# Batch 0's attention output in another pair of PSUM banks and in one piece, w_out decoded early and used split from the first chunk, splits made in place

## The chip, the cores and the metric

One core of one Trainium2 chip runs the whole kernel as one launch. The time is device time in microseconds (us); lower is better. The engines spoken of are PE (TensorE: matmuls and transposes), ACT (ScalarE), DVE (VectorE) and SP (SyncE, which issues every DMA here, in order). Each engine works through its own queue in order and waits on semaphores of the others.

## The reference, cut to what matters

```python
# attention: 2 batches, 8 heads, 768 positions, head size 64, 16 clusters per head
q_assign = argmax(q_n @ c_n.T); k_assign = argmax(k_n @ c_n.T)
mask = q_assign[..., :, None] == k_assign[..., None, :]
scores = where(mask, scale * q @ k.T, -1e9)
attn = softmax(scores); attn_out = attn @ v
x = attn_out.transpose(0, 2, 1, 3).reshape(1536, 512)
# first expert: w_in 512x2048, w_out 2048x512
h = x @ w_in
g = (a0 + a1*h + a2*h**2 + a3*h**3) / (1 + |b0|*|h| + |b1|*h**2 + 1e-6)
x = g @ w_out
# second expert: w1, w2 512x1024, w3 1024x1024, w_out 1024x512
out = ((x @ w1) * (x @ w2) @ w3) @ w_out2
```

All in fp32; the weights reach the kernel as 64-bit floats, two 32-bit words per number.

## The kernel before, in words

**Order.** The program doesn't write its order out by hand. It lists tasks (`op(engine, cost, fn, reads, writes, priority)`), and `Plan.order` places them by fixed costs over 19 rounds. The numbers in `CFG` (`AT`, `LEAD`, `OFF`, `T0` and so on) set the first round's priorities. What comes out is one order per engine and one slot for every buffer; a buffer class such as `w` has a fixed number of slots (`SLOTS`), and a new buffer waits until the slot's last user is done.

**Attention.** A head of a batch is six units (`Attn.unit`): four matmul passes give a 128x768 tile of scores in PSUM class `s` (L791), DVE takes the row maximum (L799), ACT the exponential with its sum (L800), PE turns the tile by six transposes into class `t` in two lots of three (L813), and ACT copies each lot out (L816). After six units `Attn.av` transposes the inverse sums (L833, tile R) and multiplies by v (L849, tile o), both in class `t`, whose two banks the transposes use too. The product is three tasks of four matmuls, so the planner may put other work between them. Batch masks (`masks`) come from cluster products (L415), counts (L435) and DVE passes (L426 to L438).

**Experts.** Tokens go through in four chunks of 384 columns, c = 0 to 3, each in blocks of eight 128-row steps: `p1_block` (w_in, PSUM class `s`), `p2_block` (w_out, class `m`), `p3_block` (w1 and w2, `m`), `p4_block` (w3 times w_out2, `m`). w3 times w_out2 is formed once (`FirstW`, L581, and `w_block`, L597, stored to `whd`/`wld` by `w_out_part`, L548 and L549). Chunks 0 and 1 are batch 0, chunks 2 and 3 batch 1.

**Two kinds of product.** A block of kind `D` uses the fp32 weight itself: one matmul per 128-row step, which the chip runs as two instructions (L536). Other kinds split weight and operand into a rounded high part and a low part (hi and lo, type fp32r) and make three matmuls: hi x hi, hi x lo, lo x hi (L538, L539, L540). The matrices named in `F0` are `D` in chunk 0, where w_in and w_out are used in fp32 as they come out of `decode` (ACT L466, DVE L467, L468, L470). The decoded weights are also stored to DRAM (`fin`, `fout`, `f12`); the later chunks load them (kind `S`) into a `raw` buffer, ACT rounds them to hi (L501) and DVE subtracts to get lo (L502), both in class `w`, which has 6 slots; `raw` has 3, and `p1_block`'s temporary V uses them as well.

```python
    F0=("in", "out"),
            elif k == "S":
                self.f = Buf("raw", [P, WB])
                dma(lambda: self.f.t, self.full[0], 524288, ...)
            self.hi, self.lo = Buf("w", [P, WB], F32R), Buf("w", [P, WB], F32R)
```

Of the kernel before, what the change touches and what calls it, by code (L numbers as in the profile page):

```python
# [9 lines left out]
F32 = mybir.dt.float32  # L10
# [11 lines left out]
    F0=("in", "out"),  # L22
    SPLIT=7,
    NW=(1, 3),
    AT=(0.0, 1.125, 2.5, 2.5, 3.6667, 4.0, 4.0),
    M1=0,
    LEAD=(-21.2, 10.4, -104.0),
    ALEAD=(37.3, 148.2),
    MLEAD=16.4,
    AOFF=-83.5,  # L30
    SLOTS={"w": 6, "raw": 3, "y": 3, "x": 2, "x2": 2, "g": 21, "et": 3, "E": 4, "kqr": 1, "A": 2, "B": 2, "v": 1, "sm": 6, "nn": 3, "s": 2, "t": 2, "m": 2, "sums": 2, "rb": 1},
    WO2=-2226.6,
    OFF=(-156.1, -36.7, -5.3, -214.6, -121.6, 36.6, -69.0),
# [254 lines left out]
def kernel(  # L288
# [34 lines left out]
    if not only_plan:  # L323
# [9 lines left out]
        f_d = {n: dr.tile([8, P, WB], F32, name="f" + n) for n in ("in", "out", "12")}  # L333
        ident = cst.tile([P, P], F32, name="ident")
# [138 lines left out]
    class Blk:  # L473
# [7 lines left out]
        def prep(self):  # L481
            k, at = self.kind, self.at
            pl, psp = at - cfg["LEAD"][0 if k != "L" else 1] - (0 if k == "L" else cfg["LEAD"][1]), at - cfg["LEAD"][1]
            if k in "DE":
                self.f = Buf("w", [P, WB])
                raws = [load_raw(self.src, i, at - cfg["LEAD"][2]) for i in range(2)]
                for i in range(2):
                    decode(raws[i], lambda i=i: self.f.t[:, i * HB:(i + 1) * HB], (self.f, i), psp)
                if self.full is not None:
                    dma(lambda: self.full[0](), lambda: self.f.t, 524288, [(self.f, 0), (self.f, 1)], [self.full[1]], at)  # L490
                if k == "D":
                    return
            elif k == "S":
                self.f = Buf("raw", [P, WB])
                dma(lambda: self.f.t, self.full[0], 524288, [self.full[1]], [(self.f, 0), (self.f, 1)], pl)
            self.hi, self.lo = Buf("w", [P, WB], F32R), Buf("w", [P, WB], F32R)
# [539 lines left out]
```

## Time and profile before

| | |
|---|---|
| median of 3 runs | 811.92 us (811.42 to 814.1) |
| the profiled execution's own time | 808.21 us |
| its span, first to last instruction | 806.4 us |
| busy: PE, DVE, ACT | 781.4, 608.3, 555.5 us |
| mean granted TensorE clock | 0.996 of 2.4 GHz |
| moved by DMA | 147.69 MB |

Busy time is the union of an engine's instructions; PE's matmuls overlap, so what a matmul costs is read from the distance between starts, not from its duration. A wait is idle time put down to the semaphore that came last.

### The profile page before, as it was taken

To read this page: it belongs to the slowest core of one execution; us is meant where nothing else is said; L and a number is where in the kernel's file an instruction comes from. 1 tells how busy PE (TensorE), PEld (TensorE's weight loads), DVE (VectorE), ACT (ScalarE), POOL (GpSimd) and SP (SyncE) were. 2 spreads that over 40 slices of the span, in tenths; PEclk is the share of its full clock that TensorE was granted. 3 is DMA by queue.
4 is the path that set the end of the run, shared out by engine and by line. 5 is a ranking of instruction groups with operands and counts; after the bars stand their busy time and mean duration, and the time that the engine had idled before them with its cause. 6 is when DMAs were issued, how large, how long until landed. Compare 5 with 4: busy or idle time off the path is not lost.

```text
span 806.4 us, 11425 instructions
## 1 busy us (share of the span) xinstructions
PE 781.4 (97%) x4225; PEld 638.7 (79%) x4225; DVE 608.3 (75%) x826; ACT 555.5 (69%) x943; POOL 0.7 (0%) x6
## 2 busy tenths in 40 slices
PE   5989999998989999999999999999999999999998
PEld 1446656665655667588888899999999999999998
DVE  5977888866479999779999847389967397975440
ACT  7579887877777897389988836287945386863331
POOL 0000000000000000000000000000000000000000
PEclk9999999999999999999999999999999999999999
DMA  8996747767334347973435665414475332655334
GB/s 331 323 330 183 250 154 228 247 186 235 129 109 152 101 146 236 316 261 114 161 119 162 225 211 179 143 69 151 169 250 172 105 118 94 225 186 176 130 104 145
DMA packets 54344, 147.69 MB, mean 183 GB/s; under 512 B 5904, under 2 KB 23056, under 8 KB 54288
## 3 DMA queue, kind: packets, MB, share of 16 engines
q1 hardware_dynamic: 54288, 146.96, 54.8%
q8 instruction: 33, 0.54, 0.3%
q14 instruction: 23, 0.19, 0.1%
HBM read 119.15 MB, written 24.64 MB: 178 GB/s over the span
## 4 chain that ended last, share of the span: by engine, by line
PE 80%; ACT 7%; DVE 6%; DMA 5%; issue 1%; SPq 0%; DVEq 0%; ACTq 0%
PE m L539 12%; PE m L538 12%; PE m L540 12%; PE t L849 7%; PE s L791 6%; PE t L813 6%; PE m L536 5%; PE s L538 4%; PE s L540 4%; PE s L539 4%; PE m L597 3%; PE s L536 3%; ACT E L800 1%; DMA kqr<-in_kq_dram 1%; ACT et L816 1%
## 5 line engine op out<-in xcount | busy, mean ns | idle before, releaser
L502 DVE TENSOR_TENSOR w<-raw,w 128x1024 fp32r<-128x1024 f32 x72 | 87.9, 1222 | 43.5 <-ACT w L501 42.6
L540 PE MATMUL m<-g,w 128*128 128x384 f32 x320 | 107.9, 337 | 0.0
L538 PE MATMUL m<-g,w 128*128 128x384 f32 x320 | 107.8, 337 | 0.0
L539 PE MATMUL m<-g,w 128*128 128x384 f32 x320 | 107.7, 337 | 0.0
L501 ACT CAST w<-raw 128x1024 fp32r<-128x1024 f32 x72 | 75.5, 1050 | 46.3 <-PE m L539 35.2
L816 ACT COPY et<-t 128x384 f32<-128x384 f32 x192 | 88.7, 503 | 22.0 <-PE t L813 21.9
L799 DVE TENSOR_REDUCE sm<-s 128x1 f32<-128x768 f32 x96 | 90.3, 949 | 14.0 <-PE s L791 13.8
L800 ACT ACTIVATE E<-s,sm 128x768 f32<-128x768 f32 x96 | 88.8, 929 | 10.9 <-DVE sm L799 9.7
L813 PEld LDWEIGHTS t<-ident,E 128*128 128x128 f32 x576 | 69.2, 141 | 30.5 <-issue 11.9
L813 PE MATMUL t<-ident,E 128*128 128x128 f32 x576 | 86.4, 277 | 4.4 <-ACT et L816 3.2
L538 PE MATMUL m<-x,w 128*128 128x384 f32 x256 | 87.3, 341 | 0.0
L539 PE MATMUL m<-x,w 128*128 128x384 f32 x256 | 86.3, 337 | 0.0
L540 PE MATMUL m<-x,w 128*128 128x384 f32 x256 | 85.6, 334 | 0.0
L849 PE MATMUL t<-et,v 128*64 128x384 f32 x384 | 68.5, 494 | 0.0
L538 PE MATMUL s<-x,w 128*128 128x384 f32 x192 | 66.3, 345 | 0.9 <-DVE et L657 0.9
L791 PE MATMUL s<-A 128*128 128x384 f32 x192 | 60.1, 394 | 6.2 <-ACT E L800 5.6
L540 PE MATMUL s<-x,w 128*128 128x384 f32 x192 | 64.9, 338 | 0.0
L539 PE MATMUL s<-x,w 128*128 128x384 f32 x192 | 64.4, 335 | 0.0
L466 ACT ACTIVATE y<-raw 128x512 f32<-128x512 f32 x66 | 45.5, 698 | 25.8 <-DMA raw<-in_w_out_dram 10.6
L539 PEld LDWEIGHTS m<-g,w 128*128 128x128 f32 x320 | 60.1, 188 | 0.0
L538 PEld LDWEIGHTS m<-g,w 128*128 128x128 f32 x320 | 60.1, 188 | 0.0
L540 PEld LDWEIGHTS m<-g,w 128*128 128x128 f32 x320 | 60.1, 188 | 0.0
(122 smaller groups left out, 1468.6 us busy)
## 6 DMA issues: line engine op xcount, KB each, us to landing
kqr<-in_kq_dram SPq DMA_DIRECT2D x16, 768.0 KB, 4.7
raw<-fin SPq DMA_DIRECT2D x24, 512.0 KB, 3.4
raw<-fout SPq DMA_DIRECT2D x24, 512.0 KB, 3.4
raw<-f SPq DMA_DIRECT2D x24, 512.0 KB, 3.2
raw<-in_w3t_dram SPq DMA_DIRECT2D x16, 512.0 KB, 5.9
raw<-in_w_in_dram SPq DMA_DIRECT2D x16, 512.0 KB, 4.9
raw<-in_w_out_dram SPq DMA_DIRECT2D x16, 512.0 KB, 3.9
raw<-in_w_dram SPq DMA_DIRECT2D x16, 512.0 KB, 4.7
```

What stands on the lines that cost most here:

```text
L501: op("ACT", 0.95, lambda: nc.scalar.copy(self.hi.t, self.f.t), [(self.f, 0), (self.f, 1)], [self.hi], psp)
L502: op("DVE", 1.135, lambda: nc.vector.tensor_tensor(self.lo.t, self.f.t, f32(self.hi.t), ALU.subtract), [(self.f, 0), (self.f, 1), self.hi] ...
L536: nc.tensor.matmul(o, w.f.t[:, sl], x[0], start=first, stop=last)
L538: nc.tensor.matmul(o, w.hi.t[:, sl], x[0], start=first, stop=False)
L539: nc.tensor.matmul(o, w.hi.t[:, sl], x[1], start=False, stop=False)
L540: nc.tensor.matmul(o, w.lo.t[:, sl], x[0], start=False, stop=last)
L791: nc.tensor.matmul(p.t[:, f, 0:TA], lhs.t[0:n, q0:q0 + P], lhs.t[0:n, k0:k0 + TA], start=st, stop=not st)
L799: op("DVE", 0.865, lambda: nc.vector.tensor_reduce(mx.t, p.t[:, :, 0:TA], axis=AX.XY, op=ALU.max, negate=True), [p], [mx], OF[1])
L800: op("ACT", 0.88, lambda: nc.scalar.activation(E.t, p.t[:, :, 0:TA], AF.Exp, bias=mx.t, accum_out=sums.t[:, i, j:j + 1]), [p, mx], [E, (su ...
L813: nc.tensor.transpose(t.t[:, n * P:(n + 1) * P], e[:, kt * P:(kt + 1) * P], ident)
L816: op("ACT", 0.371, lambda t=t, lot=lot: nc.scalar.copy(et.t[:, 3 * lot:3 * lot + 3, i * P:(i + 1) * P], t.t[:, 0:TA].rearrange("p (a b) -> ...
L849: nc.tensor.matmul(o.t[64 * j:64 * j + 64, 0:TA], v.t[:, kt, h % 2, :], ets[j].t[:, kt, :], start=kt == 0, stop=kt == NKT - 1)
```

## The change

It does five things. (1) `F0` loses `"out"`: chunk 0's w_out blocks become split blocks, and chunk 0's g is kept as hi and lo. (2) `PRE=("out",)`: w_out is decoded and stored to DRAM by eight blocks of its own (`early`), placed from `PT` on in the attention stage, and chunk 0 loads it back like the later chunks. (3) A split block loads its float weight into the `w` buffer that becomes lo; DVE subtracts in place, and no `raw` buffer is used. (4) `AVP=("m", "t")`: batch 0's R and o use class `m`, the expert layers' two banks, and the product with v is one task per head. (5) The priorities are other numbers. `KEEP={}` and `ETV=(0.0, 0.0)` leave their new branches unused.

```diff
-    F0=("in", "out"),
-    SPLIT=7,
-    NW=(1, 3),
-    AT=(0.0, 1.125, 2.5, 2.5, 3.6667, 4.0, 4.0),
+    F0=("in",),
+    KEEP={},
+    PRE=("out",),
+    PT=(-39.8, 52.4),
+    ETV=(0.0, 0.0),
+    AVP=("m", "t"),
+    EF="w",
+    SPLIT=8,
+    NW=(1, 4),
+    AT=(0.9167, 3.0, 3.125, 4.0, 4.0, 4.0, 4.0),
...
+            if k == "F":
+                self.f = Buf("w", [P, WB])
+                dma(lambda: self.f.t, self.full[0], 524288, [self.full[1]], [(self.f, 0), (self.f, 1)], pl)
+                return
             if k in "DE":
-                self.f = Buf("w", [P, WB])
+                self.f = f = Buf("w" if k == "D" else cfg["EF"], [P, WB])
+            if k != "D":
+                self.lo = Buf("w", [P, WB], F32R)
+            if k in "SL":
+                f = self.lo
+            words = [(f, 0), (f, 1)]
...
             elif k == "S":
-                self.f = Buf("raw", [P, WB])
-                dma(lambda: self.f.t, self.full[0], 524288, [self.full[1]], [(self.f, 0), (self.f, 1)], pl)
-            self.hi, self.lo = Buf("w", [P, WB], F32R), Buf("w", [P, WB], F32R)
+                dma(lambda: f32(f.t), self.full[0], 524288, [self.full[1]], words, pl)
+            self.hi = Buf("w", [P, WB], F32R)
...
-                op("ACT", 0.95, lambda: nc.scalar.copy(self.hi.t, self.f.t), [(self.f, 0), (self.f, 1)], [self.hi], psp)
-                op("DVE", 1.135, lambda: nc.vector.tensor_tensor(self.lo.t, self.f.t, f32(self.hi.t), ALU.subtract),
-                   [(self.f, 0), (self.f, 1), self.hi], [self.lo], psp)
+                op("ACT", 0.95, lambda: nc.scalar.copy(self.hi.t, f32(f.t)), words, [self.hi], psp)
+                op("DVE", 1.135, lambda: nc.vector.tensor_tensor(self.lo.t, f32(f.t), f32(self.hi.t), ALU.subtract),
+                   words + [self.hi], [self.lo], psp)
...
+        if c == 0 and n in cfg["PRE"]:
+            early.append(Blk("D", src, full))
+            return Blk("F" if n in F0 else "S", None, full, parts if n not in F0 and keep < NCH else None)
...
-            sums, rb, R = self.sums[h], Buf("rb", [P, NQT, P]), Buf("t", [P, 512])
+            bank = cfg["AVP"][b]
+            sums, rb, R = self.sums[h], Buf("rb", [P, NQT, P]), Buf(bank, [P, 512])
...
-            o = Buf("t", [P, 512])
+            o = Buf(bank, [P, 512])
...
-            for k0 in range(0, NKT, 2):
-                lots = {k // 3 for k in (k0, k0 + 1)}
-                op("PE", 1.31, lambda k0=k0: q(k0), [v] + [(e, l, i) for e in ets for l in lots for i in range(NQT)], [o], at)
+            op("PE", 4.06, q, [v] + [(e, l, i) for e in ets for l in range(2) for i in range(NQT)], [o], at)
```

What the change does to the order is seen at three places. In the rows, a name such as `g_2881` is a buffer of class g with a running number, `x2` counts repeats, and lines of the changed kernel are shifted (L849 becomes L883, L813 becomes L843, L799 becomes L829).

PE at the first head's product with v (`o` and R; transposes of E between): before,

```order
L833 MATMUL t_603<-ident,rb_594 128x128 x3
L849 MATMUL t_611<-et_492,v_318 64x384
L849 MATMUL t_611<-et_552,v_318 64x384
L849 MATMUL t_611<-et_492,v_318 64x384
L849 MATMUL t_611<-et_552,v_318 64x384
L813 MATMUL t_619<-ident,E_581 128x128 x3
L849 MATMUL t_611<-et_492,v_318 64x384
L849 MATMUL t_611<-et_552,v_318 64x384
L849 MATMUL t_611<-et_492,v_318 64x384
L849 MATMUL t_611<-et_552,v_318 64x384
```

and in the changed kernel:

```order
L867 MATMUL m_703<-ident,rb_694 128x128 x3
L843 MATMUL t_711<-ident,E_680 128x128 x3
L843 MATMUL t_715<-ident,E_680 128x128 x3
L883 MATMUL m_719<-et_564,v_429 64x384
L883 MATMUL m_719<-et_645,v_429 64x384
L883 MATMUL m_719<-et_564,v_429 64x384
L883 MATMUL m_719<-et_645,v_429 64x384
L883 MATMUL m_719<-et_564,v_429 64x384
```

The transposes of E no longer stand inside the product, R and o have moved from the `t` banks to `m`, and over the whole order the product is in 16 stretches where it was in 30.

DVE just ahead of the first row maximum (TENSOR_REDUCE of `sm`), before,

```order
L470 SCALAR_TENSOR_TENSOR x_381<-w_310,y_378 128x512
L470 SCALAR_TENSOR_TENSOR w_420<-raw_365,y_399 128x512
L549 TENSOR_TENSOR raw_448<-t_236,w_439 128x512
L799 TENSOR_REDUCE sm_453<-s_434 128x1
L799 TENSOR_REDUCE sm_458<-s_443 128x1
```

and in the changed kernel, where L433 to L445 are mask work and L474, L477 decoding:

```order
L433 TENSOR_TENSOR g_493<-g_461,s_452 128x768
L477 SCALAR_TENSOR_TENSOR x_404<-w_397,y_443 128x512
L445 SCALAR_TENSOR_TENSOR g_431<-s_476,g_418 128x768
L434 STREAM_TRANSPOSE g_499<-g_493 128x768
L474 TENSOR_SCALAR y_491<-y_491 128x512
L435 TENSOR_REDUCE nn_514<-g_499 128x48
L829 TENSOR_REDUCE sm_518<-s_502 128x1
L829 TENSOR_REDUCE sm_522<-s_509 128x1
```

Nine of batch 1's twelve DVE mask passes now stand ahead of the first row maximum; before they all stood far behind it (batch 0's twelve are ahead in both). On PE, the cluster products of batch 1 and one of its two counts have moved there too, and 28 of `FirstW`'s 32 matmuls stand ahead of the first unit where 30 did.

PE in chunk 0's w_out blocks (`g` times `w` into `m`), before,

```order
L536 MATMUL m_2989<-g_2227,w_2954 128x384 x2
L536 MATMUL m_2989<-g_2318,w_2954 128x384 x2
L536 MATMUL m_2989<-g_2411,w_2954 128x384 x2
L536 MATMUL m_2989<-g_2477,w_2954 128x384 x2
L536 MATMUL m_2989<-g_2549,w_2979 128x384 x2
```

and in the changed kernel:

```order
L568 MATMUL m_3344<-g_2881,w_3371 128x384
L569 MATMUL m_3344<-g_2897,w_3371 128x384
L570 MATMUL m_3344<-g_2881,w_3298 128x384
L568 MATMUL m_3344<-g_2881,w_3371 128x384
L569 MATMUL m_3344<-g_2897,w_3371 128x384
L570 MATMUL m_3344<-g_2881,w_3298 128x384
```

One matmul per step has become three, with a second g buffer and a second w buffer. The slots that the order gives to class `w` have moved as well: among the last 64 blocks that ACT and DVE split, the slot for hi is free one PE block ahead of its first matmul for 53 and two blocks ahead for 11, and the slot for lo three blocks ahead for 51. Before, both slots were mostly free two blocks ahead.

## Rows read from the trace of the kernel before

**Rows 1.** The page's first part: busy time, share of the span and instructions of each engine.

```profile
PE 781.4 (97%) x4225; PEld 638.7 (79%) x4225; DVE 608.3 (75%) x826; ACT 555.5 (69%) x943; POOL 0.7 (0%) x6
```

**Rows 2.** Busy time by stage: the stretch, its length, then busy us and instructions of PE, PE's weight loads, DVE, ACT and POOL, granted TensorE clock, DMA share and GB/s.

```profile
0.00:58.00 58.00, 46.54 (x159) 19.65 (x160) 44.00 (x83) 38.66 (x60) 0.70 (x6) 0.97 0.95 335
58.00:84.00 26.00, 24.67 (x144) 17.55 (x143) 20.19 (x29) 25.65 (x58) 0.00 (x0) 1.00 0.65 191
...
177.00:203.00 26.00, 22.05 (x121) 15.26 (x120) 18.11 (x28) 20.81 (x47) 0.00 (x0) 0.93 0.76 237
...
240.00:322.00 82.00, 81.66 (x371) 54.22 (x370) 78.03 (x110) 69.23 (x125) 0.00 (x0) 1.00 0.49 155
322.00:347.00 25.00, 25.00 (x95) 13.99 (x94) 19.81 (x33) 9.58 (x15) 0.00 (x0) 1.00 0.93 310
347.00:445.00 98.00, 95.86 (x581) 83.15 (x580) 90.72 (x125) 86.28 (x156) 0.00 (x0) 1.00 0.49 159
445.00:803.00 358.00, 358.00 (x2057) 354.96 (x2055) 240.78 (x284) 203.25 (x281) 0.00 (x0) 1.00 0.47 159
```

**Rows 3.** The chain that ended last, one piece of chunk 0's w_out blocks (start us, length us, what, instructions); and PE's groups by line and shape: instructions, then busy us and mean ns of one.

```profile
321.24 19.35 PE m L536 x60
```

```profile
L536 PE MATMUL m<-g,w 128*128 128x384 f32 x128 | 43.6, 486 | 0.0
```

**Rows 4.** Timeline of PE around the end of one split block and the whole next one (start us, length us, engine, line, operation, tiles, shape, count): L539 is the last reader of a block's hi.

```profile
479.80 0.34 PE L539 MATMUL m<-g,w 128*128 128x384 f32 x1
...
480.15 0.34 PE L538 MATMUL s<-x,w 128*128 128x384 f32 x1
...
484.36 0.34 PE L538 MATMUL m<-g,w 128*128 128x384 f32 x1
```

**Rows 5.** Timeline of PE at two heads' products with v: one in two pieces with a lot of transposes between, one in a single piece.

```profile
67.06 1.51 PE L849 MATMUL t<-et,v 128*64 128x384 f32 x8
68.50 0.55 PE L813 MATMUL t<-ident,E 128*128 128x128 f32 x3
68.98 2.80 PE L849 MATMUL t<-et,v 128*64 128x384 f32 x16
71.71 0.55 PE L813 MATMUL t<-ident,E 128*128 128x128 f32 x3
...
84.32 4.09 PE L849 MATMUL t<-et,v 128*64 128x384 f32 x24
88.34 0.62 PE L791 MATMUL s<-A 128*128 128x384 f32 x2
```

**Rows 6.** The start on DVE: busy time of DVE in a stretch (its length, busy us and instructions, then clock and DMA), then its timeline at the first row maxima, where square brackets give idle time and who ended it.

```profile
10.44:49.30 38.86, 38.45 (x68) 0.96 0.97 358
```

```profile
48.66 0.70 DVE L470 SCALAR_TENSOR_TENSOR w<-raw,y 128x512 uint32<-128x512 uint32 x1
52.59 0.69 DVE L549 TENSOR_TENSOR raw<-t,w 128x512 fp32r<-128x512 f32 x1 [3.24 <-ACT w L548]
53.20 1.81 DVE L799 TENSOR_REDUCE sm<-s 128x1 f32<-128x768 f32 x2
```

**Rows 7.** Pieces of the chain that ended last: batch 1's cluster products and counts, and `FirstW`'s matmuls (two instructions each).

```profile
21.56 1.72 PE t L581 x4
...
109.45 1.43 PE s L415 x16
...
116.95 1.29 PE s L435 x4
```

**Rows 8.** Who waited for whom from 184 to 190 us (us in total, times, longest), and single microseconds of the same stretch in the columns of the table by stage.

```profile
DVE w L470 <- DMA whd<-w: 3.5, 1, 3.5
...
PE s L791 <- ACT E L800: 2.5, 2, 2.1
```

```profile
188.00:189.00 1.00, 0.47 (x1) 0.47 (x2) 0.96 (x3) 1.00 (x4) 0.00 (x0) 0.70 0.01 4
189.00:190.00 1.00, 1.00 (x5) 0.90 (x5) 0.64 (x1) 0.55 (x2) 0.00 (x0) 0.50 1.07 283
190.00:191.00 1.00, 1.00 (x6) 1.00 (x5) 0.79 (x1) 0.82 (x3) 0.00 (x0) 0.50 1.09 197
191.00:192.00 1.00, 1.00 (x6) 1.00 (x5) 0.17 (x1) 0.81 (x2) 0.00 (x0) 0.59 0.82 188
```

**Rows 9.** Timeline of ACT and of DVE where one block's weight is split: ACT waits for the slot of hi, then rounds; DVE subtracts.

```profile
480.17 1.05 ACT L501 CAST w<-raw 128x1024 fp32r<-128x1024 f32 x1 [2.75 <-PE m L539]
```

```profile
481.25 1.22 DVE L502 TENSOR_TENSOR w<-raw,w 128x1024 fp32r<-128x1024 f32 x1 [2.08 <-ACT w L501]
```

**Rows 10.** DVE's groups by line and shape (instructions, then busy us and mean ns of one): the three passes of a decode, and the split of g.

```profile
L468 DVE SCALAR_TENSOR_TENSOR y<-raw,y 128x512 uint32<-128x512 uint32 x66 | 45.0, 685 | 0.7
L470 DVE SCALAR_TENSOR_TENSOR w<-raw,y 128x512 uint32<-128x512 uint32 x64 | 43.7, 686 | 10.0 <-DMA whd<-w 3.5 <-PE s L536 2.3 <-DMA f<-w 2.2
...
L467 DVE TENSOR_SCALAR y<-y 128x512 uint32<-128x512 uint32 x72 | 30.0, 419 | 9.9 <-ACT y L466 9.8
L530 DVE TENSOR_TENSOR g<-et,g 128x768 fp32r<-128x768 f32 x24 | 22.9, 953 | 1.8 <-ACT g L528 1.8
```

**Rows 11.** DMA issues of the page: engine queue, operation, count, KB each, median us from issue to landing.

```profile
raw<-fout SPq DMA_DIRECT2D x24, 512.0 KB, 3.4
```

More of the change, by code (lines that the diff above doesn't have):

```diff
@@ L333 @@
         f_d = {n: dr.tile([8, P, WB], F32, name="f" + n) for n in ("in", "out", "12")}
+        s_d = {n: dr.tile([2, 8, P, WB], F32, name="s" + n) for n in ("in", "out", "12")}
         ident = cst.tile([P, P], F32, name="ident")
@@ L510, in cost @@
         def cost(self, n):
-            return n * (0.645 if self.kind == "D" else 0.523)
+            return n * (0.645 if self.kind in "DF" else 0.523)
     def moe_blk(c, n, i, src):
         full = (lambda: f_d[n][i], ("f", n, i))
-        if c == 0:
-            return Blk("D" if n in F0 else "E", src, full)
-        return Blk("S", None, full)
+        parts = tuple((lambda j=j: s_d[n][j, i], [("s", n, i, j)]) for j in range(2))
+        keep = cfg["KEEP"].get(n, 9)
+        if c == 0 and n in cfg["PRE"]:
+            early.append(Blk("D", src, full))
+            return Blk("F" if n in F0 else "S", None, full, parts if n not in F0 and keep < NCH else None)
+        if c == 0:
+            if n in F0:
+                return Blk("D", src, full)
+            return Blk("E", src, full if keep > 1 else None, parts if keep < NCH else None)
+        if c >= keep:
+            return Blk("L", None, None, parts)
+        return Blk("S", None, full, parts if n in F0 and c == 1 and keep < NCH else None)
+    early = []
     def operand(n, cls, shape, c):
@@ L815, in unit @@
                 op("PE", 0.327, tr, [E], [t], OF[3])
[L816 to L818 removed]
+                u, part = 6 * h + qt, cfg["ETV"][self.b]
+                on_dve = lot == 1 and int(part * (u + 1)) > int(part * u)
+                op("DVE" if on_dve else "ACT", 0.43 if on_dve else 0.371,
+                   lambda t=t, lot=lot, v=on_dve: (nc.vector.tensor_copy if v else nc.scalar.copy)(
+                       et.t[:, 3 * lot:3 * lot + 3, i * P:(i + 1) * P], t.t[:, 0:TA].rearrange("p (a b) -> p a b", a=3)),
+                   [t], [(et, lot, i)], OF[4])
             if qt == 2 * NQT - 1:
@@ L842, in av, with q @@
             op("PE", 0.327, tr, [rb], [R], at)
-            o = Buf("t", [P, 512])
+            o = Buf(bank, [P, 512])
             ets = [self.et[h, 0], self.et[h, 1]]
-            def q(k0):
-                for kt in range(k0, k0 + 2):
+            def q():
+                for kt in range(NKT):
                     for j in range(2):
@@ L914 @@
         clock += tm + ta
+    for i, b in enumerate(early):
+        b.at = cfg["PT"][0] + i * cfg["PT"][1]
+        events.append((b.at, 1, "pre", b))
     events.sort(key=lambda e: (e[0], e[1]))
@@ L919, with decode_early @@
     mask_at = {e[3]: e[0] for e in events if e[2] == "mask"}
-    state = {"b": 0, "h": 0, "u": 0, "m": []}
+    state = {"b": 0, "h": 0, "u": 0, "e": 0, "m": []}
+    def decode_early(key):
+        for b in early[state["e"]:]:
+            if key is not None and ("f", *key) in plan.wr:
+                break
+            b.prep()
+            state["e"] += 1
+            if key is None:
+                break
     def prep_blocks(i):
         while state["b"] <= min(i, len(blocks) - 1):
+            if blocks[state["b"]].kind in "FS":
+                decode_early(blocks[state["b"]].full[1][1:])
             blocks[state["b"]].prep()
```

38 lines of the change are left out of this document (21 added, 17 removed).

## The prediction

> **What bounds the kernel now.** I read the page's busy shares first: PE is busy 781.4 us of a span of 806.4, DVE 608.3, ACT 555.5 [rows 1]. So the question is always what PE does, and what it waits for. The table by stage says where the 25 us without PE lie [rows 2]. From 445 to 803 us PE is busy for all of 358.00 us at full clock: chunks 1 to 3 are nothing but PE, and only less PE work can shorten them. The start, 0 to 58, has 11.5 us without PE and a clock of 0.97. The stretch 177 to 203 has 4.0 us and a clock of 0.93, 58 to 84 has 1.3, 347 to 445 has 2.1; about 2 lie in a stretch that the rows leave out, and the rest after 803, where the last tile is copied and stored. In between, 240 to 347, PE is busy, but DVE is too: 78.03 of 82.00 us and 19.81 of 25.00.
>
> Two things follow. Work taken from PE after 58 us comes off the end nearly in full, since PE has almost no idle time there into which it could vanish. And work given to DVE or ACT costs nothing as long as it finds a place beside PE; DVE has the least room.
>
> The sum is made against the profiled execution's own 808.21 us. The median of the runs is 811.92, so I scale the result by 811.92 / 808.21 = 1.0046. A difference under about 0.3%, 2.4 us, is what a measurement of this kernel can't tell from none.
>
> **1. Chunk 0's w_out blocks become split blocks.** In fp32, 60 instructions took 19.35 us on the chain, 0.3225 us each; the eight blocks have 128, that is 16 or 5.16 us a block [rows 3]. A split block has 24 matmuls. The one that starts at 480.15 is followed by the next at 484.36: 4.21 us [rows 4]. The saving is 0.95 us a block, 8 x 0.95 = **7.6 us**. At 240 to 347 PE is the engine that waits least, so I take all of it; the other bound is nothing (third rival).
>
> What it adds beside PE: eight casts and eight subtractions of weights, 1.05 us on ACT and 1.22 on DVE [rows 9], and the split of eight tiles of g, 0.95 on DVE [rows 10] and about the same on ACT. That is 17.4 us more for DVE, at most 16 for ACT. What leaves the same stretch: the 16 decodes of w_out, each 0.42 + 0.69 + 0.69 = 1.8 us of DVE by duration [rows 10], about 29 us. DVE has 97.8 of 107 us now in 240 to 347 [rows 2], so it should have a little more room than before. The decodes go to the attention stage, where DVE has 5.8 us of 26 free in 58 to 84 and 7.9 of 26 in 177 to 203 [rows 2]. I cost both at nothing, with PE's own work as the cover; if the cover were gone, a decode would cost its 1.8 us. The eight extra loads of 512 KB each land in 3.4 us [rows 11], and the DMA share is 0.49 in most of that stretch; without cover, 3.4 us a block, 27 in all, but they depend only on stores made long before.
>
> **2. The product with v in one piece.** A product cut in two took 1.44 us (67.06 to 68.50) and 2.73 (68.98 to 71.71), 4.17 together; one in a single piece took 4.02 (84.32 to 88.34) [rows 5]. A cut costs 0.15 us, and the order has 30 stretches now and 16 after: 14 x 0.15 = **2.1 us**. Bounds: nothing, if the cuts filled waits; 4.6, if the lone transposes in the cuts (0.48 us from 68.50 to 68.98, against 0.30 from 71.71 to the next start) are counted too. That batch 0's R and o sit in the `m` banks leaves both `t` banks to the transposes. I give that no price: it can only spare waits, which are the stretches named under 4.
>
> **3. The start.** DVE is busy 38.45 of 38.86 us from 10.44 to 49.30 [rows 6]: it paces the start. Then it sits 3.24 us behind one subtraction that waits for ACT, and the first row maximum starts at 53.20. In the changed order nine mask passes of batch 1 stand ahead of that maximum, and the subtraction (0.61 us) stands behind it. A pass of this size takes 0.9 us (two in 1.81) [rows 6], so DVE arrives at 49.3 + 9 x 0.9 + 0.3 for a first decode pass that also moves ahead = 57.7, **4.5 us later**. PE uses that time: four sets of cluster products of 1.43, a count of 1.29, less two of `FirstW`'s matmuls at 0.86 (1.72 for two) [rows 7], 4 x 1.43 + 1.29 - 1.72 = 5.3 us of work that no longer stands at 100 to 128, where it was all PE's time. Net **-0.8 us**. Bounds: -5.3, if the passes fit into DVE's idle 3.24 us and the wait for data; +6, if the subtractions of w_out_part, which now follow closely and write into `raw` slots that a store has just read, each wait 3.5 us as the one DVE wait on such a store did [rows 8]. Queued behind them are the next units' row maxima, and PE waits for those.
>
> **4. The wait at 184 to 190.** DVE sat 3.5 us until the store `whd<-w` had landed, ACT behind DVE, and PE 2.1 us behind ACT [rows 8]. The clock fell after it: 0.70, 0.50, 0.50, 0.59 in four microseconds, a loss of 0.3 + 0.5 + 0.5 + 0.41 = 1.7 us. With the shorter waits around it, the stretch 177 to 203 lost 4.0 us idle and 1.8 of clock, 5.8 [rows 2]. The new order has no such stretch at that place, but more stores of decoded weights, each a chance for the same. I take a third of the 5.8 as gained, **-2.0**; bounds -5.8 and nothing.
>
> **5. Splits in place.** A split block now needs only two `w` slots and no `raw`, but lo is taken from the start of the load, so hi's slot comes free later: one block ahead for 53 of 64 blocks, where it was two. What must fit into that one block: the last reader of hi starts at 479.80, the next block at 480.15 [rows 4]; ACT's cast starts at 480.17, 1.05 us, DVE's subtraction at 481.25, 1.22 us [rows 9], done at 482.47. That is 2.3 us after the slot came free, 2.6 with a semaphore's way to PE, against 4.21. There are 1.6 us to spare. I take **+1.0** for blocks at which both engines come late together. Bounds: nothing, and 24 (first rival).
>
> Here a rule of the Trainium skill speaks against the change. First the row: after a wait of 2.1 us the clock went to 0.50 and 1.7 us were lost, while in 58 to 84 waits of 1.3 us in all left it at 1.00 [rows 2, 8]. The page "TensorE: Matmul & The Clock Gate", section "A second HAM failure mode: psum-queue depth-cycling", says that many small idle times between groups of matmuls can make the clock fall and rise again and again. By that rule a small wait at every block would cost more than itself; by the rows it would not, as long as each is short. The sum goes by the rows, and the rule is the fourth rival.
>
> **The sum.** -7.6 - 2.1 - 0.8 - 2.0 + 1.0 = -11.5 us: 808.2 becomes 796.7, and times 1.0046 **800.4 us**, 1.4% faster.
>
> **The rivals.** *First, slower: PE waits for hi at the block's head.* In the stages where p1 blocks alternate with p3 blocks, ACT and DVE also run the long chain of the rational function, passes of about 1 us. If one stands ahead of the cast and one ahead of the subtraction, 2.3 + 0.3 + 2 = 4.6 us don't fit into 4.21: 0.45 us a block, 53 blocks, 24 us, so 808.2 - 12.5 + 24 = 819.7, scaled 823. It decides from 12.5 / 53 = 0.24 us a block. For it: DVE's load in 240 to 322. Against: over 445 to 803 DVE is busy 240.78 of 358 us and ACT 203.25 [rows 2], and the order can put the cast first. Chance 0.10.
>
> *Second: the start gives back what it gains.* Terms 3 and 4 become +6 and 0: -7.6 - 2.1 + 6 + 1.0 = -2.7, 805.5, scaled 809. For it: DMA share 0.95 and DVE full at the start. Chance 0.13.
>
> *Third: the change doesn't do what it says.* DVE at 95% in 240 to 322 delays g's parts, PE waits as long as it saved, and term 1 is nothing: -3.9, 804.3, scaled 808. Against: DVE loses more there than it gets. Chance 0.10.
>
> *Fourth: the clock.* One fall of 1.7 us in each of the nine eight-block stages of chunks 1 to 3 is 15.4 us: 812.1, scaled 816. No row shows a fall without a wait of 2 us. The skill's page named above is what speaks for it. Chance 0.03.
>
> **How the numbers follow.** The forecast has 0.64. Faster by over 0.3%: the forecast, most of the third rival and about half of the second, 0.79. Slower: the first and the fourth, 0.13. The rest, 0.08, within 0.3%. The range's low end takes the good bounds of 3, 4 and 5, -7.6 - 2.1 - 5.3 - 5.8 = -20.8, 787.4, scaled 791. The high end, 811, takes in the second and third rivals and leaves out the first and fourth; with something below 791, that leaves about 0.17 outside.
>
> **What the next profile would show.** Term 1: chunk 0's w_out blocks as L568 to L570 with starts 0.175 us apart and no wait of PE for `w` or `g`. Term 2: 16 pieces of 24 instructions at 4.02 us. Term 3: the first row maximum at about 57.7 us, the first exponential near 59. Term 4: no clock under 0.9 between 60 and 440. Term 5: PE still busy without a gap in chunks 1 to 3, each L501 (now L517) waiting for PE. What would make the forecast wrong: PE waits on `w` from DVE in chunks 1 to 3, or a first head that is later than 62 us.

## The result and the profile after

The changed kernel took 792.62 us in the median of 4 runs (791.17 to 793.23), the kernel before 811.67 beside it (809.49 to 814.1): a ratio of 0.9762, with a 95% interval of 0.9731 to 0.9793. The time lies in the range of 791 to 811, 7.8 us under the forecast of 800.4. About half of that miss is the choice of base. The two profiled executions took 808.21 and 793.23 us, 15.0 apart, where the sum said 11.5. The medians are 19.0 apart, because the profiled execution of before lay 3.5 us under its median and that of after 0.6 over its own; scaling by 1.0046 added the scatter of single executions to the forecast. The result lies 1.6 us inside the range's low end; two neighbouring orders of the changed kernel, measured below, lie at 799.7 and 802.1, close to the forecast.

The page of the changed kernel, busy time by engine and the chain that ended last by engine:

```profile
PE 763.6 (96%) x4289; PEld 648.1 (82%) x4289; DVE 621.3 (79%) x842; ACT 566.3 (72%) x959; POOL 0.7 (0%) x6
...
PE 68%; DVE 15%; ACT 9%; DMA 5%; issue 3%; SPq 0%; ACTq 0%; DVEq 0%
```

The same row of the chain on the page of before:

```profile
PE 80%; ACT 7%; DVE 6%; DMA 5%; issue 1%; SPq 0%; DVEq 0%; ACTq 0%
```

PE is busy 17.8 us less [rows 1], and idle 27.9 us instead of 25.0. More of the chain now runs through DVE. Busy time by stage, after, in the columns of [rows 2]:

```profile
0.00:58.00 58.00, 43.83 (x206) 18.32 (x207) 47.19 (x86) 42.63 (x62) 0.70 (x6) 1.00 0.89 319
58.00:84.00 26.00, 24.30 (x132) 16.58 (x132) 22.71 (x32) 23.48 (x51) 0.00 (x0) 1.00 0.80 239
84.00:177.00 93.00, 89.55 (x522) 63.00 (x521) 75.05 (x118) 81.82 (x180) 0.00 (x0) 1.00 0.72 228
177.00:240.00 63.00, 61.42 (x331) 39.66 (x330) 52.32 (x79) 51.74 (x106) 0.00 (x0) 1.00 0.81 266
240.00:322.00 82.00, 78.73 (x401) 57.33 (x401) 76.21 (x98) 71.01 (x123) 0.00 (x0) 1.00 0.45 146
322.00:347.00 25.00, 24.79 (x158) 21.40 (x157) 24.84 (x40) 25.00 (x54) 0.00 (x0) 1.00 0.74 231
347.00:445.00 98.00, 97.91 (x589) 89.03 (x589) 91.15 (x126) 78.63 (x131) 0.00 (x0) 1.00 0.50 165
445.00:790.00 345.00, 343.07 (x1961) 342.76 (x1959) 231.87 (x271) 192.01 (x262) 0.00 (x0) 1.00 0.46 160
```

and of before, the two stretches that [rows 2] leave out or cut:

```profile
84.00:177.00 93.00, 93.00 (x533) 57.97 (x532) 72.87 (x109) 74.47 (x153) 0.00 (x0) 1.00 0.66 212
177.00:240.00 63.00, 56.65 (x298) 37.20 (x297) 41.90 (x58) 47.89 (x100) 0.00 (x0) 0.97 0.53 165
```

In after the clock column is 1.00 in every row; for the first microseconds that is no measurement (last section). The stretch 177 to 240 changed most: 33 more PE instructions, 4.8 us less idle. In 240 to 322 PE has 3.3 us idle where it had 0.3, and in 322 to 347 DVE and ACT are as full as PE.

Since PE's matmuls overlap and a short wait can hide behind one still running, I also add up distances between starts. For each kind of instruction I take its usual distance to the next start as its work (a split matmul 0.174 us, fp32 0.323, scores 0.178, transposes 0.109, the product with v 0.168, each from runs of starts without a wait); what a distance has beyond it is loss, with the time before PE's first start. The split into work and loss is mine; the sum is the span. Stages are stretches of time, and the same work can stand in another stage of the other kernel. The last column is the part of the loss that lies between a transpose of E and the next start, whatever starts next, but for mask and `FirstW` matmuls.

| us | span | work | loss | 0–84 | 84–177 | 177–240 | 240–347 | 347–445 | from 445 | loss at transposes |
|---|---|---|---|---|---|---|---|---|---|---|
| before | 806.4 | 755.5 | 50.9 | 22.3 | 2.8 | 13.2 | 2.3 | 4.9 | 5.3 | 9.6 |
| after | 791.5 | 747.6 | 43.8 | 20.4 | 6.5 | 3.5 | 6.1 | 1.4 | 6.0 | 3.0 |
| difference | −14.9 | −7.9 | −7.1 | −1.9 | +3.7 | −9.7 | +3.8 | −3.5 | +0.7 | −6.6 |

So half of the gain is PE work that is gone, and half is waiting that is gone, most of it between 177 and 240 us and, by the instruction, most of it behind transposes. There the next start is either the next lot of transposes (7.4 us of loss before, 4.1 after) or a score matmul (3.2 before, none after), which waits for the exponential. PE's waits, after (us in total, times, longest):

```profile
PE t L393 <- DVE E L391: 13.3, 1, 13.3
PE s L821 <- ACT E L830: 4.1, 6, 1.6
PE t L843 <- ACT et L849: 1.5, 1, 1.5
```

and before, where transposes into `t` waited for the copy that frees the bank (L843 and L849 are now what L813 and L816 were):

```profile
PE s L415 <- ACT g L409: 6.2, 1, 6.2
PE s L791 <- ACT E L800: 5.6, 8, 2.1
PE t L813 <- ACT et L816: 3.2, 5, 1.3
```

Two of these waits in before's timeline of PE, in a stretch of which the prediction did not speak:

```profile
236.26 0.55 PE L813 MATMUL t<-ident,E 128*128 128x128 f32 x3 [1.28 <-ACT et L816]
237.46 0.55 PE L813 MATMUL t<-ident,E 128*128 128x128 f32 x3 [0.66 <-ACT et L816]
```

Neither has to do with R or o. ACT had copied that head's R by 223.6, and DVE read its o at 227.01; from then on both `t` banks held transposes alone. ACT came late with its copies (L816), because passes of the rational function (L653, L655) stood between them:

```profile
227.01 0.55 DVE L857 TENSOR_TENSOR E<-t,rb 128x384 f32<-128x384 f32 x1
...
235.03 0.81 ACT L653 ACTIVATE et<-s 128x768 f32<-128x768 f32 x1 [0.65 <-DVE et L656]
235.73 0.47 ACT L816 COPY et<-t 128x384 f32<-128x384 f32 x1
236.09 0.95 ACT L655 ACTIVATE raw<-et,abc 128x768 f32<-128x768 f32 x1
236.93 0.48 ACT L816 COPY et<-t 128x384 f32<-128x384 f32 x1
```

Of before's five waits of transposes for such a copy one, 0.3 us at 183.90, came while R stood in a `t` bank, and none while o did.

### The profile page after: what moved, and what is told of

The parts are those of the page before. It is cut to its first block, busy times and chain, and to the rows that moved or that the text cites. A ratio compares the mean times of both kernels' runs of the same rounds, so it can differ in the third digit from the quotient of the medians.

```text
span 791.5 us, 11624 instructions
## 1 busy us (share of the span) xinstructions
PE 763.6 (96%) x4289; PEld 648.1 (82%) x4289; DVE 621.3 (79%) x842; ACT 566.3 (72%) x959; POOL 0.7 (0%) x6
## 4 chain that ended last, share of the span: by engine, by line
PE 68%; DVE 15%; ACT 9%; DMA 5%; issue 3%; SPq 0%; ACTq 0%; DVEq 0%
PE m L570 14%; PE m L568 14%; PE m L569 14%; PE s L568 4%; PE s L570 4%; PE s L569 4%; PE s L821 4%; PE t L843 3%; ACT E L830 3%; PE t L883 3%; PE m L883 3%; DVE sm L829 2%; ACT et L849 2%; DVE y L475 2%; PE m L627 2%
## 5 line engine op out<-in xcount | busy, mean ns | idle before, releaser
L518 DVE TENSOR_TENSOR w<-w,w 128x1024 fp32r<-128x1024 f32 x88 | 106.5, 1219 | 66.1 <-ACT w L517 64.4
L517 ACT CAST w<-w 128x1024 fp32r<-128x1024 f32 x88 | 91.9, 1057 | 88.2 <-PE m L569 67.7
L568 PE MATMUL m<-g,w 128*128 128x384 f32 x384 | 130.4, 340 | 0.0
L569 PE MATMUL m<-g,w 128*128 128x384 f32 x384 | 129.2, 336 | 0.6 <-DVE g L560 0.6
L570 PE MATMUL m<-g,w 128*128 128x384 f32 x384 | 129.2, 336 | 0.0
L849 ACT COPY et<-t 128x384 f32<-128x384 f32 x192 | 87.8, 507 | 10.5 <-PE t L843 8.0
L829 DVE TENSOR_REDUCE sm<-s 128x1 f32<-128x768 f32 x96 | 90.2, 948 | 5.3 <-PE s L821 5.1
L843 PE MATMUL t<-ident,E 128*128 128x128 f32 x576 | 84.1, 275 | 2.9 <-ACT et L849 1.5
L570 PE MATMUL m<-x,w 128*128 128x384 f32 x256 | 86.3, 337 | 0.0
L843 PEld LDWEIGHTS t<-ident,E 128*128 128x128 f32 x576 | 68.4, 140 | 21.1 <-issue 6.4
L569 PEld LDWEIGHTS m<-g,w 128*128 128x128 f32 x384 | 72.1, 188 | 1.0 <-DVE g L560 0.9
L568 PEld LDWEIGHTS m<-g,w 128*128 128x128 f32 x384 | 72.1, 188 | 0.1
L570 PEld LDWEIGHTS m<-g,w 128*128 128x128 f32 x384 | 72.1, 188 | 0.0
L570 PE MATMUL s<-x,w 128*128 128x384 f32 x192 | 64.7, 337 | 0.0
L821 PE MATMUL s<-B 80*128 80x384 f32 x192 | 49.5, 339 | 1.0 <-DMA B<-A 1.0
```

What stands on the lines that cost most here:

```text
L517: op("ACT", 0.95, lambda: nc.scalar.copy(self.hi.t, f32(f.t)), words, [self.hi], psp)
L568: nc.tensor.matmul(o, w.hi.t[:, sl], x[0], start=first, stop=False)
L569: nc.tensor.matmul(o, w.hi.t[:, sl], x[1], start=False, stop=False)
L570: nc.tensor.matmul(o, w.lo.t[:, sl], x[0], start=False, stop=last)
L821: nc.tensor.matmul(p.t[:, f, 0:TA], lhs.t[0:n, q0:q0 + P], lhs.t[0:n, k0:k0 + TA], start=st, stop=not st)
L829: op("DVE", 0.865, lambda: nc.vector.tensor_reduce(mx.t, p.t[:, :, 0:TA], axis=AX.XY, op=ALU.max, negate=True), [p], [mx], OF[1])
```

## The experiments

There were four questions: whether PE's work still sets the end (term 1), which part of the change carries the gain, how much room the in-place splits have (term 5), and how far any one order can be trusted, since every edit but a few also moves the planner's order. "Own order" below means that the kernel's order stayed as it was; otherwise the planner made a new one from the same numbers.

### What one order is worth

One priority number moved by 1, nothing else:

```diff
-    AOFF=42.2,      # after
+    AOFF=43.2,      # e_nudge;  41.2 in e_nudge2
-    AOFF=-83.5,     # before
+    AOFF=-82.5,     # e_bnudge
```

> The changed kernel with one priority number moved by one (AOFF 43.2 for 42.2): the same work and the same buffers in a slightly different order, with 50 to 140 places of difference on each engine. It measures how far the time hangs on the order alone. Theory (work and banks make the gain): within 5 us of 792.6. Rival (the gain is mostly that this order was picked): 798 or more.

> The changed kernel with the same priority number moved by one the other way (AOFF 41.2): a second sample of what a new order alone does. If the first nudge is typical: 798 to 806. If the scatter is as wide as the effects under test: above 808 or at 793 and below.

> The kernel before with one priority number moved by one (AOFF -82.5 for -83.5): the same work in a slightly different order. Theory: within 5 us of 811.7, so that a single order tells little of a change under 5 us. Rival: the order of before was unlucky at one place (the wait on a store at 184 us, 5.8 us with the clock), and any other order saves it: 805 to 807.

Measured: e_nudge 802.06 us (ratio to before 0.9862, 0.9847 to 0.9877), e_nudge2 799.70 (0.984, 0.9798 to 0.9882), e_bnudge 820.65 (1.0093, 1.0077 to 1.0108). Both kernels are better than their neighbours, by 7 to 9 us, with the same instructions. The loss rises from 43.8 to 53.1 and 49.3 (transposes 6.7 and 9.3) and from 50.9 to 63.7 (transposes 14.7). In e_nudge part of it is the clock: its profile has a mean of 0.994, that of after and of e_nudge2 1.000, and 0.006 of 800.8 us is at most some 4.8 us (an estimate). That bounds what the next experiments can say: a kernel with a new order is compared with the nudged orders as well as with its parent, and a difference under about 10 us is not read as the part's own. The neighbours of the two kernels are still 18.6 and 21.0 us apart, about as far as the kernels themselves: the gain is not only a lucky order.

### PE's work in chunk 0: less and more, in the same order

e_drop leaves out chunk 0's third w_out matmul, lo x hi:

```diff
+        part = w.src is None and w.c0out
-        nc.tensor.matmul(o, w.hi.t[:, sl], x[1], start=False, stop=False)
-        nc.tensor.matmul(o, w.lo.t[:, sl], x[0], start=False, stop=last)
+        nc.tensor.matmul(o, w.hi.t[:, sl], x[1], start=False, stop=last and part)
+        if not part:
+            nc.tensor.matmul(o, w.lo.t[:, sl], x[0], start=False, stop=last)
```

> The changed kernel in its own order on every engine, but without the third matmul (lo x hi) of chunk 0's w_out blocks: 64 matmuls of about 0.174 us, 11.1 us of PE work, are left out, and with them that part of chunk 0's result. Theory: PE sets the end, so work taken from it in this stage comes off nearly in full: 9 to 11 us less than the changed kernel's 792.6, 781.5 to 783.5. Rival: DVE, 95% busy in this stage, sets its pace, and PE's work vanishes into waits: less than 4 us, 789 or more.

e_fp32same makes each of these steps one fp32 matmul on the high parts, as long on PE as in before:

```diff
+        if w.c0out:
+            nc.tensor.matmul(o, f32(w.hi.t[:, sl]), f32(x[0]), start=first, stop=last)
+            return
```

> The changed kernel in its own order on ACT, DVE and SP, and on PE but for chunk 0's w_out blocks: there the three split matmuls of a step are one fp32 matmul again (two instructions), on the high parts of g and w_out, so the low parts are left out of chunk 0's result; the passes that make them still run. PE gets 7.6 us more work. Leaving out 11.1 us of PE work in the same place gave nothing, so DVE and ACT pace this stage in the changed kernel. If PE is just below them: 0 to 4 us more than the changed kernel's 792.6. If the split is where the gain of the change came from, PE becomes the bound again: 6 to 8 us more, 799 to 801.

e_dropg leaves out hi x lo instead, and with it DVE's subtraction that makes g's low part in chunk 0:

```diff
-            op("DVE", cd, lambda: nc.vector.tensor_tensor(ap(dst[1].t), src(), f32(ap(dst[0].t)), ALU.subtract),
+            op("DVE", cd, (lambda: None) if drop else lambda: nc.vector.tensor_tensor(...),
-        nc.tensor.matmul(o, w.hi.t[:, sl], x[1], start=False, stop=False)
+        if not w.c0out:
+            nc.tensor.matmul(o, w.hi.t[:, sl], x[1], start=False, stop=False)
```

> The changed kernel in its own order, without the eight DVE subtractions that make the low part of g in chunk 0 and without the 64 matmuls that read it (hi x lo): 7.6 us less on DVE and 11.1 us less on PE, and chunk 0's result lacks that part. The run without lo x hi took the same 11.1 us from PE and left DVE alone. If DVE paces the stage: 4 to 8 us less than the changed kernel, 785 to 789. If the order's chain through the attention units paces it whatever DVE does: within 2 us of 792.6.

Measured: e_drop 793.34 us (0.9759, 0.9741 to 0.9777), so 11.1 us less PE work gave nothing in the median and 3.4 us between the spans of the profiled executions. e_fp32same 800.21 (0.9846, 0.9805 to 0.9886): 7.6 us more work cost 7.6 (6.8 by the ratios). e_dropg 791.41 (0.9734, 0.970 to 0.9768): 1.2 us less (2.3 by the ratios), with DVE relieved as well. The stretch 240 to 322 and the chain by engine, first e_drop:

```profile
240.00:322.00 82.00, 76.07 (x376) 52.48 (x375) 76.20 (x99) 70.99 (x123) 0.00 (x0) 1.00 0.46 144
...
PE 52%; DVE 23%; ACT 12%; DMA 7%; issue 5%; SPq 0%; DVEq 0%; ACTq 0%
```

then e_fp32same:

```profile
240.00:322.00 82.00, 79.72 (x362) 52.00 (x361) 75.30 (x96) 69.93 (x120) 0.00 (x0) 1.00 0.45 142
...
PE 68%; DVE 13%; DMA 8%; ACT 8%; issue 2%; SPq 1%; ACTq 0%; DVEq 0%
```

In e_drop DVE and ACT do in this stretch exactly what they do in after (76.2 and 71.0 us) and PE just sits longer; DVE's share of the chain goes from 15% to 23%. In e_fp32same PE fills up again. So the changed kernel stands at the knee: PE's work sets the end when 7.6 us of it are added, but the next 11.1 us taken away meet the chain of row maximum, exponential and the p1 passes on DVE and ACT. e_dropg speaks for a chain and against DVE's amount of work, since eight subtractions less gave little in the same order.

### Each part undone in the changed kernel

Batch 0's R and o back in the transposes' banks; w_out back to fp32 in chunk 0 without early decoding; and splits through `raw` again:

```diff
-    AVP=("m", "t"),        # e_tt
+    AVP=("t", "t"),
-    F0=("in",),            # e_fp32
+    F0=("in", "out"),
-    PRE=("out",),
+    PRE=(),
-            if k in "SL":          # e_raw
+            if k == "S":
+                f = self.f = Buf("raw", [P, WB])
+            if k == "L":
```

> The changed kernel with AVP (t, t): batch 0's R and o back in the transposes' banks, everything else kept, the order made anew. The trace has PE's transposes losing 6.6 us less to waits than before. A new order alone cost 9.4 us when one priority was nudged. If the banks matter on top of that: 802 + 6, 806 to 812. If they don't: 798 to 804.

> The changed kernel with w_out in F0 and PRE empty: chunk 0's w_out blocks in fp32, decoded where they are used, as in the kernel before; banks, single product, splits in place and numbers are kept, the order made anew. If the split with the early decode carries the change: 810 to 816. If it carries little: 798 to 804, as the nudged order.

> The changed kernel with splits not in place: a split block loads into a raw buffer again, hi and lo are two more buffers of class w, as in the kernel before; all else and the numbers kept, the order made anew. If splits in place are worth something beyond a new order (802): above 806. If they are neutral, as the unbroken PE row of chunks 1 to 3 in both kernels suggests: 798 to 806.

Measured: e_tt 809.62 us (0.997, 0.995 to 0.9991), e_fp32 810.78 (0.9978, 0.9956 to 1.0001), e_raw 823.45 (1.0131, 1.0091 to 1.017). Above the nudged orders (799.7 and 802.1) that is 8 to 10, 9 to 11 and 21 to 24 us. By the measure of 10 us above, only e_raw is clear of the scatter of orders. PE's waits in e_tt, in e_nudge and e_nudge2, and from 445 us on in e_raw:

```profile
PE t L843 <- ACT et L849: 6.5, 9, 1.4
PE s L821 <- ACT E L830: 6.1, 15, 1.0
```

```profile
PE t L843 <- ACT et L849: 5.0, 7, 1.5
...
PE t L843 <- ACT et L849: 4.8, 6, 1.6
```

```profile
PE m L572 <- DVE w L520: 2.7, 2, 2.0
PE s L572 <- DVE w L520: 2.7, 3, 1.4
```

In e_tt the loss at transposes is 17.0 us (after 3.0, nudged 6.7 and 9.3). That the shared banks cost this is not shown, and the traces speak against it. Of e_tt's nine waits for ACT's copy one, 0.7 us at 113.72, came while R stood in a `t` bank, and none while o did; and the nudged orders, whose batch 0 has R and o in `m`, have 5.0 and 4.8 us of the same wait, more than before with its 3.2. In e_raw the loss from 445 us on is 19.5 instead of 6.0; PE waits there for the low part of a weight (L520 is the subtraction), in stages that had no wait. The clock takes part too: e_raw's profile has a mean of 0.983, and 0.017 of 821.2 us is 14 us at most (an estimate), where e_nudge has 4.8 by the same working. Whether `raw` itself does this, or only these priorities, which suit blocks that need no `raw`, is open: no order was looked for with it.

### Single parts in the kernel before

e_bav: the banks and the one-piece product alone. e_bsplit: w_out split in chunk 0 alone, with its decoding left where it was.

```diff
-            sums, rb, R = self.sums[h], Buf("rb", [P, NQT, P]), Buf("t", [P, 512])      # e_bav
+            sums, rb, R = self.sums[h], Buf("rb", [P, NQT, P]), Buf("mt"[b], [P, 512])
-            o = Buf("t", [P, 512])
+            o = Buf("mt"[b], [P, 512])
-            for k0 in range(0, NKT, 2):
...
+            op("PE", 4.06, q, [v] + [(e, l, i) for e in ets for l in range(2) for i in range(NQT)], [o], at)
-    F0=("in", "out"),                                                                   # e_bsplit
+    F0=("in",),
```

> The kernel before with one part of the change alone: batch 0's R and o in the m banks and the product with v as one task per head, order made anew by the numbers of before. The nudged kernel before took 820.6, and its transposes lost 14.7 us beyond their own length, 9.6 in before and 3.0 in the changed kernel. If the banks carry over: 805 to 813, with the transposes' loss at 8 or less. If their gain needs the other parts: 817 to 824.

> The kernel before with w_out taken out of F0 and nothing else: chunk 0's w_out blocks are split blocks, decoded where they are used (no early decode), order made anew. PE has 7.6 us less to do; DVE gets 16 passes more in a stage where it is 95% busy and the decodes stay there. If the saved PE work counts by itself: 811 to 815 against the nudged 820.6. If it needs the early decode to make room on DVE: 818 to 824.

Measured: e_bav 826.82 us (1.017, 1.012 to 1.0219), e_bsplit 820.95 (1.009, 1.0058 to 1.0122). Neither part brought anything alone in the one order measured of each; against the nudged before (820.65) one is 6 us slower and one equal. In e_bav R and o stand in `m`, and yet the loss at transposes is 16.5 us, where 8 or less was expected if the banks carried over (before 9.6, e_bnudge 14.7). PE's waits, e_bav and then e_bsplit:

```profile
PE s L791 <- ACT E L800: 12.4, 12, 3.5
```

```profile
PE s L791 <- ACT E L800: 10.7, 10, 2.6
PE t L813 <- ACT et L816: 6.8, 9, 1.9
```

e_bsplit has exactly the changed kernel's PE work, 747.6 us, and a loss of 69.5: the 7.9 us came back as waits for the exponential and for the transposes' copies. That looks like the third rival with the decoding left in chunk 0, where DVE is full, but it is not shown: e_bnudge, in fp32, loses as much in 240 to 347 (13.8 us, e_bsplit 13.7), and e_bsplit's excess over it lies mostly in 347 to 445 (9.5 against 3.5).

### The room of a split block

The cast to hi is made twice, in the own order; ACT gets 1.05 us more in every split block:

```diff
-    lambda: nc.scalar.copy(self.hi.t, f32(f.t))
+    lambda: (nc.scalar.copy(self.hi.t, f32(f.t)), nc.scalar.copy(self.hi.t, f32(f.t)))
```

> The changed kernel in its own order, but ACT rounds every split block's weight to hi twice, into the same buffer: 88 casts of 1.05 us more on ACT, each ahead of DVE's subtraction. Theory of the prediction: a block has 1.6 us to spare between hi's slot coming free and its first matmul, so 0.95 us more costs little: 0 to 5 us. Rival (the order in which hi is free only one block ahead has no room): PE waits about 0.5 us or more a block, 40 us or more in all.

Measured: 818.77 us (1.0065, 1.0037 to 1.0092), 26 us more than after. Neither expectation held: it cost more than waits here and there would, less than the whole cast at every block. The wait that was not there in after, and the stretch in which most of its instances lie:

```profile
PE m L570 <- DVE w L518: 6.7, 11, 0.8
...
445.00:600.00 155.00, 149.67 (x842) 146.29 (x842) 121.81 (x141) 125.67 (x161) 0.00 (x0) 1.00 0.46 158
```

The room can be read from one block of after, in the timelines of PE, ACT and DVE:

```profile
561.10 0.34 PE L568 MATMUL m<-x,w 128*128 128x384 f32 x1
...
565.32 0.34 PE L568 MATMUL s<-x,w 128*128 128x384 f32 x1
```

```profile
561.30 1.05 ACT L517 CAST w<-w 128x1024 fp32r<-128x1024 f32 x1 [1.13 <-PE s L570]
```

```profile
562.91 1.22 DVE L518 TENSOR_TENSOR w<-w,w 128x1024 fp32r<-128x1024 f32 x1
```

PE's next block starts 4.22 us after this one. The cast starts 0.20 us into it, but the subtraction does not follow at 562.35: DVE is in the rational function until 562.9, and is done at 564.13. If the weight is for the next block, as it is for 53 of 64, 1.2 us are to spare, or 1.5 up to the low part's first reader, the block's third matmul (L570). Another 1.05 us of cast would end at 563.40 and move the subtraction back by some 0.5 (an estimate), so that 0.7 and 1.0 are left here; where one more pass of about 1 us stands ahead, PE waits.

## Why the prediction came out as it did

**Direction, and term 1 (−7.6): right, in size too.** PE's work is 7.9 us less, and e_fp32same gives back 7.6 in full. Chunk 0's w_out steps do stand 0.175 us apart: 333.33, 333.50, 333.68, 333.86, 334.04 in PE's timeline. They waited once, 0.6 us for `g`. The sentence ahead of it, that "work taken from PE after 58 us comes off the end nearly in full", held for these 7.6 us alone. The next 11.1 gave nothing, and I had no way of knowing from busy shares how far it would hold; the row of 240 to 322 with DVE at 78 of 82 us [rows 2] said that there was an end to it.

**Term 2 (−2.1): right for the pieces; the banks' price of nothing is not refuted.** The 16 pieces take 4.02 us each, as the two below do (75.90 to 79.92 and 325.31 to 329.33), and the loss at the product with v went from 2.1 to 0.0:

```profile
75.90 4.09 PE L883 MATMUL m<-et,v 128*64 128x384 f32 x24
79.92 0.62 PE L821 MATMUL s<-A 128*128 128x384 f32 x2
...
325.31 4.09 PE L883 MATMUL t<-et,v 128*64 128x384 f32 x24
329.33 0.55 PE L843 MATMUL t<-ident,E 128*128 128x128 f32 x3
```

The sentence on the banks, "I give that no price: it can only spare waits, which are the stretches named under 4", fits the waits that the traces show: the one wait of before with R in a `t` bank, 0.3 us, lies in that stretch, and e_bav and e_tt show no gain or cost of the banks that the order could not make. The most that the traces show of shared banks is small: two of e_bnudge's ten such waits, 1.3 us, came with o in a `t` bank, and one wait in e_fp32, 1.1 us ahead of 244.11, was for R itself, of batch 1, whose R and o the change leaves in `t`. What the sum lacked is a term for the waits of transposes, and of the score matmuls behind them, outside that stretch, such as those at 236 and 237. In all, the loss at transposes was 9.6 us and fell by 6.6. That belongs to this order: the nudged orders have 6.7 and 9.3 with the same banks. Why this order has less is open.

**Term 3 (−0.8): the delay nearly as worked out, the net not settled.** The first row maximum came at 58.35 us (57.7 forecast):

```profile
58.35 1.80 DVE L829 TENSOR_REDUCE sm<-s 128x1 f32<-128x768 f32 x2
```

Of the four subtractions of w_out_part that I feared one waited for a store, 1.4 us ahead of 74.24, so the bad bound of +6 was not reached. What PE got back can't be separated: the loss up to 84 us is 1.9 lower, that from 84 to 177 is 3.7 higher.

**Term 4 (−2.0): mis-sized.** The wait at 184 to 190 and its fall of the clock are gone; I gave a third of 5.8. The larger stretch 177 to 240 lost 13.2 us before and 3.5 after, 9.7 less. Of that, 3.7 us lie between 203 and 240, which the rows that I went by leave out, and where PE stood behind ACT's copies out of `t`; and in 177 to 203 the loss was 8.5 before, where I had 5.8, and 2.5 after. Part of it is the loss at transposes named under term 2, so the two can't be added.

**Term 5 (+1.0): the condition right, the sign open.** From 445 us on the loss is 6.0 us (before 5.3), and no wait of PE stands there: the first rival did not occur. But in the block shown above the room up to the next block is 1.2 us, not 1.6, since DVE comes late, and e_cast2 shows that one more cast uses it up at some blocks. The 0.3 us for "a semaphore's way to PE" stands in no row: at 236.26 above PE starts 0.06 us after ACT's copy ends. And undoing the in-place splits under the new priorities cost 21 us or more. As these priorities came with the change, that may say that the parts belong together, and not that `raw` is dear.

**What the sum left out.** In 240 to 347 the loss rose by 3.8 us as PE became quicker than the chain beside it; in 347 to 445 it fell by 3.5. I had both at nothing, and they cancel. The stages together, −1.9 + 3.7 − 9.7 + 3.8 − 3.5 + 0.7, are −6.9, and with −7.9 of work −14.8, the difference of the spans but for rounding.

**The clock.** No stretch of after shows a fall of the granted clock, so the fourth rival did not occur. What the changed kernel gained of clock in its profile is the fall after 188 us, some 1.8 us [rows 2]; the 0.97 of 0 to 58 is no gain (last section). In the medians it is probably more: in 35 executions of before that ran beside the experiments the mean granted clock was 0.989 to 0.998, with a median of 0.994, in the four of after 0.998 to 1.000. But the sentence "No row shows a fall without a wait of 2 us" does not hold: in before itself the clock fell at 14 us after a wait of 1.84, and in e_fp32 PE waited 1.11 us before 244.11 and 0.35 before 245.01, and then there came this fall:

```profile
240.00:246.00 6.00, 4.54 (x24) 3.06 (x21) 5.09 (x7) 4.00 (x7) 0.00 (x0) 1.00 0.85 259
246.00:250.00 4.00, 4.00 (x12) 2.49 (x11) 3.62 (x6) 3.97 (x8) 0.00 (x0) 0.57 0.26 70
```

That is 1.7 us lost. On the other side e_cast2's stretch 445 to 600, with 5.3 us of idle time and no wait over 0.8, kept 1.00. The Trainium skill, "TensorE: Matmul & The Clock Gate", section "A second HAM failure mode: psum-queue depth-cycling", says that many small idle times can make the clock swing; e_fp32 agrees as far as waits well under 2 us go, e_cast2 does not as far as the repetition goes.

**What stays open.** How much of the 19 us belongs to each part: parts put back one by one cost more together than the whole, and parts taken alone gave nothing. Each was measured with one order, and one order is uncertain by 7 to 9 us. Shown in one and the same order are only the 7.6 us of PE work; the rest goes with the new order as a whole. The change also moves five of the eight raw halves of `FirstW`'s w_out2 to other buffer classes (`WR`), which no run tests alone.

## What to carry to other kernels

When PE is busy 97% of the span, a cut in its work pays only until the chain beside it is as long; leaving out a further piece of PE's work, and adding one, in the same order tells on which side of that point a kernel stands. Before a wait for a PSUM bank is put down to the bank's other tenant, look whether that tenant stood in it then: here R or o did at one of five waits before and at one of nine in e_tt, and the others stood behind late copies. Where a planner makes the order, first measure a neighbouring order of each kernel: here that scatter (7 to 9 us) was nearly half of the effect, and single parts of the change on the old priorities were slower than the kernel before.

## What was not expected of the hardware

**An earlier first matmul brought nothing.** In before PE's first matmuls start at 6.16 us, in after at 13.28, and at 20 us both had lost about as much (14.8 us before, 15.1 after, in the sums above). The first matmuls were slow in both. The first 16 cluster matmuls in before, the first 16 in after, and 16 of the same kind in after later on (duration in ns: least, median, most; then first and last start):

```profile
L415 PE MATMUL s<-g,bones x16: 486/847/849, 6.2 to 11.2; 128*32 128x384 f32 x16
```

```profile
L422 PE MATMUL s<-g,bones x16: 847/847/849, 13.7 to 15.6; 128*32 128x384 f32 x16
...
L422 PE MATMUL s<-g,bones x16: 486/486/510, 47.1 to 48.1; 128*32 128x384 f32 x16
```

At 13.7 the sixteen starts take 1.9 us, at 47 they take 1.0: PE ran there at half pace, as at the lower of the clock's two levels (1.2 and 2.4 GHz), though the clock column of after says 1.00. That trace's first record of the clock is at 17.15 us (in before at 10.91), and where there is no record the column shows 1.00. Before had the slow start behind it at 11 us, but then PE stood idle for 1.84 us ahead of 13.55, and the clock fell once more; after went through it once. First before, then after:

```profile
12.00:14.00 2.00, 0.30 (x1) 0.14 (x1) 2.00 (x6) 2.00 (x4) 0.00 (x0) 1.00 1.04 406
14.00:16.00 2.00, 1.21 (x2) 0.70 (x3) 1.93 (x5) 2.00 (x5) 0.00 (x0) 0.58 1.01 405
```

```profile
12.00:14.00 2.00, 0.72 (x5) 0.39 (x9) 1.97 (x5) 1.35 (x4) 0.00 (x0) 1.00 1.05 419
14.00:16.00 2.00, 2.00 (x16) 0.59 (x12) 1.74 (x4) 1.30 (x3) 0.00 (x0) 1.00 0.95 332
```

The second fall does not come with the early start alone: e_nudge also starts at 5.7 us, and its clock stays at 1.00 from 12 to 20.

**An idle time does not fix what the clock does.** In e_bsplit a wait of 2.63 us that ended at 262.80 left it at 1.00 to 280, and one of 1.89 that ended at 279.74 was followed by 0.50 from 282 to 286. It fell after 2.1 us in before and within a wait of 3.5 in e_bav, stayed at 1.00 after 1.9 in e_drop, and fell after 1.1 and 0.35 in e_fp32. So a forecast from "the wait is longer than 2 us" is a guess.
